# First norm's modulation in column blocks, with products against a 64-fold vector

## Chip, cores, metric

One core of one Trainium2 chip runs the whole kernel. The metric is device time in microseconds of one execution; about 1% is what a measurement of this kernel can tell from no change. Engines are named as in the profile: PE multiplies matrices (PEld is its loading of the stationary operand), DVE, ACT and POOL work on vectors, and SP issues nearly all transfers.

## The reference, cut to what matters

A block of a transformer with conditioned norms. A vector `c` of 512 gives six rows of modulation through `w_mod` (512 x 3072); the first norm uses the first two of them, a shift `sa` and a scale `ca`.

```python
mod = (_silu(c) @ w_mod).reshape(c.shape[0], 6, 1, -1)
sa, ca, ga, sb, cb, gb = (mod[:, i] for i in range(6))
h = _layernorm(x) * (1 + ca) + sa              # x: 1 x 2048 x 512
x = x + ga * _A_ref(h, wq, wk, wv, wo, beta)   # 32 heads, 4 segments of 512, with a memory
h = _layernorm(x) * (1 + cb) + sb
x = x + gb * _B_ref(h, w1, b1, w2, b2)         # 512 -> 1792 -> 512, squared relu
```

Inside `_A_ref` the first step is `q = h @ wq`, `k = h @ wk`, `v = h @ wv`.

## The kernel before

All work is written as nodes of a plan: `op(engine, cost, function, priority, after, get, put)`. Every engine has a hand-kept list `ORDER` of node numbers, and the plan sends each engine's instructions in the order of that list. An engine therefore waits at the head of its list even if something behind it could go. Synchronization between engines follows the tiles that instructions read and write.

The sequence is cut in four segments of 512 tokens. For the first one the start of the kernel goes like this.

- `silu` forms the vector `cs`, four columns of 128. Around it PE runs fillers (L566), products of zeros of 512 columns which compute nothing.
- `mod_cols` makes the scale. `mod_parts` loads 128 rows of `w_mod` at a time (L581), multiplies them with `cs` into four row groups (L588), ACT copies the row (L592), and four one-column products turn it into columns (L608), read out by DVE (L610).
- `mod_first` makes the shift. It loads four row blocks (L618) and makes four one-column products with each (L623), every 128 x 128 piece of `w_mod` being stationary once. DVE sums the parts (L629).
- `ln1` loads x (`load_x`, L698), takes statistics (L637, L638), finds the reciprocal deviation on POOL (L645, L646) and normalizes on DVE (L649).
- `ln_transposed` turns 256 tokens at a time (L658): PE transposes four 128 x 128 pieces a step into two PSUM banks, and an affine step applies scale and shift per channel, one chunk of 128 channels on ACT (L670) and the next on DVE (L672). The result is split into a high half (ACT, L678) and a low half (DVE, L680) of `HT`. Chunks 0 and 1 form one pair, chunks 2 and 3 the other. Every affine step waits for all of the scale and the shift (`MODC`).
- `split_w` loads `wk`, `wq` and `wv` (L740), the first 128 columns of each on their own, and splits them into halves (ACT L750, POOL or DVE L754).
- `qk(0)` is the first projection, three products per step (L786 to L788): for each of `wq` and `wk` and each half of the tokens four steps, one per channel chunk. The first step of a half waits for all four parts of `HT` of those tokens.
- Copies of the result (L833, L835) go to the tile `ST` by twelve transfers (L850), from which the scores (L908) are formed. The other groups of projections (L796), the memory and the value products follow, then the output projection and the second half of the block (L1514 to L1577).

Of the kernel before, what the change touches and what calls it, by code (L numbers as in the profile page):

```python
# [8 lines left out]
F32 = mybir.dt.float32  # L9
# [4 lines left out]
ALU = mybir.AluOpType  # L14
# [4 lines left out]
P = 128  # L19
D = 512  # L20
# [40 lines left out]
16 56 37 40 24 43 17 58 3 27 59 46 36 55 25 61 29 20 31 19 71 50 33-34 73 42 22 76 57 78 41 80 91 82 92 35 49 52 51  # L61
103 53 21 26 18 104 23 30 156 146 157 147-148 158-159 149 160 150-152 161 153 162-163 32 54 39 47-48 44 312-315 45 60
317-320 215 731-732 28 38 743-744 220 181 225 182-184 470-473 234 186 242 187-188 228 189 244 475-476 223 477-478
198-200 230 201 340 247 203-204 253 205-206 258 265 595-598 239 261 273 600-601 268 348 602-603 350 353 249 277 359
345 278 256 279 281 288 411 284 355 291 369 414 382 498 511 296 384 506 536 372 300-302 416 753 423 390 431 367 754
426 755-756 364 508 419 758-759 503 760 374 761 517 530 398 435-436 439 442 539 437 400 392 513 446 449 522 406 623
631 856 454 408 527 636 458-460 525 541 924 548 925 544 926 532 551 927 642 650 929 556 930-931 628 932 661 633
560-562 564 784-785 571 574 786-787 567 655 789 579 790 652 791 638 647 792 993 818 583-585 664 657 666 673 1061 669
1062 837 1063 831 1064 676 845 1066-1067 828 681 1068 860 1069 823 1346-1347 685-687 1358-1359 689 801-802 826 696 803
692 804 699 704 806-807 842 833 808 955 850 809 968 708-710 847 866 1198 873 1199 881 852 1200-1201 876 974 963  # L70
1203-1204 869 1205-1206 960 987 1130 885-887 863 889 965 979 896 892 997 970 899 1267 984 904 908 1092 1100 982
909-910 1003 1006 1105 989 1010 1013 1000 1097 1018 1022 1102 1368 1111 1023-1024 1026 1119 1369 1033 1370 1041 1371
1036 1029 1373 1124 1374 1107 1375 1229 1121 1376 1116 1045-1047 1399 1140 1400-1401 1143 1402 1134 1147 1404 1155
1242 1405 1126 1406 1150 1237 1407 1248 1159 1137 1234 1163 1160-1161 1166 1253 1539 1170 1540 1271 1541 1178 1239
1542 1471 1544 1173 1545 1258 1546 1244 1547 1433 1446 1274 1182-1184 1277 1261 1284 1961-1962 1973-1974 1292
1416-1417 1256 1418-1419 1280 1287 1421 1263 1422 1452 1441 1423-1424 1438 1608 1460 1296-1298 1457 1300 1676 1307
1677 1443 1303 1678-1679 1310 1465 1315 1681-1682 1448 1683 1475 1684 1570 1462 1319-1321 1478 1481 1578 1488
1813-1814 1491 1467 1815-1816 1589 1583 1484 1818-1819 1602 1496 1745 1820 1575 1612 1821 1580 1615 1500 1599 1504
1501 1507 1502 1511 1597 1514 1585 1519 1707 1882 1594 1523 1717 1618 1621 1524-1525 1720 1625 1604 1628 1712 1749
1633 1715 1726 1637-1639 1641 1648 1983 1739 1984 1656 1985 1722 1986 1644 1651 1734 1988-1990 1844 1857 1991 1849  # L80
1660-1661 1752 1662 2011 1852 1755 2012-2014 1762 1765 1854 2016-2017 1770 1731 2018 1859 2019 1736 1863 2145-2146
2083 1758 1873 2147-2148 1876 1868 2150-2151 1741 2152-2153 2045 1871 1774-1776 1778 2028 1781 2029 1785 1878 2030
1788 2031 1793 2064 2033 2058 1797-1799 1892 1899 2034 2050 2035-2036 1907 2053 2273-2274 1902 2275 2055 2276 2211
2278 2077 1895 2279 2069 2280 2060 2281 2074 2192 1911-1913 2072 1915 1922 1918 2205 1925 1930 2079 2197 1934 2173
2087 2200 1935-1936 2094 2097 2401 2178 2402-2404 2102 2090 2183 2406-2407 2186 2408-2409 2181 2339 2106 2188 2110
2113 1886 2107 2202 2117 2108 2120 2125 2301 2309 2129 1889 2215 2218 2314 2130-2131 2222 2207 2311 2225 2230 2320
2325 2234 2467 2235-2236 2238 2241 2306 2550-2553 2245 2248 2330 2561-2564 2316 2253 2328 2429 2333 2257-2259 2439
# [25 lines left out]
1 12 72 125 115 97 93 99 95 109 105 111 107 127 117 139 137 154 164 141 129 119 166 135 217 733 216 737 745 749 321
323 131 325 235-236 194 196 190-191 195 197 479 192-193 481 483 231-232 342 121 255 341 254 214 212 259 207 213 266
210-211 260 208-209 267 262 275 263 274 269-270 747 251 250 751 735 739 604 606 360 608 361 283 282 289 412-413 290
356 280 285-286 293 292 357 383 499 298 297 500 537-538 303 14 418 417 424-425 391 432-433 428 427 421 420 375-376 519
518 762 399 764 767 441 444 440 443 438 401 769 515 514 448 447 450-451 624 407 857 455-456 625 409 858 461 543 542
550 549 545 533-534 553 552 546 643 557-558 644 933 662 935 663 938 563 565-566 940 573 576 572 575 568-569 581 580
640 639 800 797 793 799 796 995 819 794 798 795 994 820 586 659 658 668 675 674 670 667 671 838-839 678 677 683 861
682 1070 862 1072 1075 1348 1352 688 1077 1364 690 1360 691 698 697 694 693 700-701 705-706 835 834 957 812 814  # L120
816-817 810 956 813 811 711 815 868 867 874-875 883 853 882 854 877 975 878 976 870-871 1207 1209 1350 1362 1131-1132
# [278 lines left out]
def block_kernel(ctx, tc, x, wq, wk, wv, wo, beta, w1, b1, w2, b2, c, wmod, out):  # L400
# [201 lines left out]
    def mod_cols(m, slot, plus, pr, after=(), pool="xr"):  # L602
# [3 lines left out]
        def mm():  # L606
            for k in range(KD):
# [3 lines left out]
                   pr + 0.05, after=[n], put=[b])  # L611

    def mod_first(m, slot, plus, pr):

        key, b = ("wmod", m), ("modc", m)
        n = None
        for k in range(KD):
# [1015 lines left out]
```

## Time and profile before

| what | value |
|---|---|
| median of 3 runs | 765.24 us (764.63 to 771.92) |
| profiled execution | 768.07 us |
| its span | 766.3 us |
| mean granted clock | 0.982 |
| PE busy | 739.7 us, 97% |
| DVE, ACT, POOL busy | 599.8, 501.1, 253.5 us |
| first projection begins | 23.38 us after the span's start |

In the profile's rows the first number is the start within the span and the second the time that the row took; a row can merge several neighbouring instructions, whose number stands behind the x. A name such as `bmodc` is a PSUM bank. What stands in brackets is the engine's idle time before the row and what ended it.

### The profile page before, as it was taken

The page shows a single profiled execution, that of the slowest core. Times are in us where ns is not written, and L with a number is a line of the kernel's source. Part 1 is how long each engine was busy: PE and PEld are TensorE (multiplying, and loading weights), DVE is VectorE, ACT ScalarE, POOL GpSimd, SP SyncE. Part 2 cuts the span into 40 slices and gives each one's busy share as a digit, 9 for nine tenths or more (in the row PEclk, how much of TensorE's full clock was granted, in tenths as well). Part 3 has the DMA queues.
Part 4 walks back from the last instruction along what each step waited for, and adds up shares of the span by engine and source line. Part 5 has one row for each costly group of instructions (what it writes and reads, how often), then busy time and mean ns, then how long its engine had stood idle before and what let it go on. Part 6 is the DMA issues. An engine that isn't in the chain of part 4 may idle for free.

```text
span 766.3 us, 17131 instructions
## 1 busy us (share of the span) xinstructions
PE 739.7 (97%) x6107; PEld 574.9 (75%) x6107; DVE 599.8 (78%) x1460; ACT 501.1 (65%) x977; POOL 253.5 (33%) x351
## 2 busy tenths in 40 slices
PE   9998999999999999999999599999999999999998
PEld 6776657776777667765565488889889898899886
DVE  4686788878997888688967999999968676776543
ACT  1547778889887896787867445667566455654541
POOL 4537245447765675565757230100000000000000
PEclk8999899999999999999999799999999999999999
DMA  9665667536665676658787868636533335233401
GB/s 304 176 153 131 191 182 219 151 100 172 187 182 149 187 201 167 179 154 223 224 226 228 257 207 278 193 127 198 165 123 115 114 110 165 66 108 123 124 1 56
DMA packets 102143, 126.72 MB, mean 165 GB/s; under 512 B 18981, under 2 KB 54569, under 8 KB 102058
## 3 DMA queue, kind: packets, MB, share of 16 engines
q1 hardware_dynamic: 101906, 125.49, 55.5%
q8 instruction: 49, 0.80, 0.4%
q14 instruction: 36, 0.29, 0.1%
q10 hardware_dynamic: 152, 0.13, 0.1%
HBM read 70.59 MB, written 27.99 MB: 129 GB/s over the span
## 4 chain that ended last, share of the span: by engine, by line
PE 77%; DVE 7%; ACT 5%; SPq 4%; issue 3%; DMA 2%; POOL 0%; DVEq 0%; ACTq 0%; POOLq 0%
PE bqk L796 8%; PE bpv L1127 6%; PE bpf L1577 6%; PE bpf L1576 6%; PE bpf L1575 6%; PE bv L875 5%; PE ba L908 5%; PE bpb L1068 5%; PE bhy L1514 3%; PE bhy L1516 3%; PE bhy L1515 3%; ACT pt L1085 3%; PE bhx L1516 3%; PE bhx L1514 3%; PE bhx L1515 2%
## 5 line engine op out<-in xcount | busy, mean ns | idle before, releaser
L913 DVE CUSTOM_DVE_ANT_0 ba<-ba,msk 128x384 f32<-128x384 f32 (+2 forms) x384 | 186.3, 542 | 40.0 <-PE ba L908 33.5
L1085 ACT ACTIVATE pt<-bpb 128x512 f32<-128x512 f32 x320 | 170.8, 615 | 23.9 <-PE bpb L1068 20.9
L796 PE MATMUL bqk<-HT,WQK 64*128 64x512 f32 x720 | 100.0, 397 | 0.2 <-DVE phi L843 0.2
L1072 POOL TENSOR_SCALAR_AFFINE_SELECT pt<-pt 128x512 f32<-128x512 f32 x128 | 79.5, 643 | 58.4 <-ACT pt L1085 52.2
L1460 ACT CAST ST<-SG 128x768 fp32r<-128x768 f32 (+1 forms) x56 | 52.3, 941 | 60.0 <-PE bhy L1515 56.4
L1577 PE MATMUL bpf<-W,ST 128*128 128x512 f32 x224 | 88.8, 396 | 0.5 <-DVE ST L1562 0.5
L1575 PE MATMUL bpf<-W,ST 128*128 128x512 f32 x224 | 88.9, 397 | 0.0
L1576 PE MATMUL bpf<-W,ST 128*128 128x512 f32 x224 | 88.6, 395 | 0.0
L1068 PE MATMUL bpb<-ST 64*128 64x256 f32 (+2 forms) x512 | 77.8, 351 | 6.6 <-DVE mx L913 1.8
L1127 PE MATMUL bpv<-pt,VT 128*32 128x512 f32 (+3 forms) x1024 | 79.3, 437 | 1.5 <-POOL pt L1072 0.7
L796 PEld LDWEIGHTS bqk<-HT,WQK 64*128 64x128 f32 x720 | 69.7, 185 | 12.4 <-issue 1.7
L908 PE MATMUL ba<-ST 63*128 63x256 f32 (+2 forms) x512 | 76.5, 349 | 0.9 <-DMA ST<-SG 0.3
L1068 PEld LDWEIGHTS bpb<-ST 64*128 64x128 f32 x512 | 51.8, 187 | 27.3 <-issue 4.4
L1463 DVE TENSOR_TENSOR ST<-SG,ST 128x768 fp32r<-128x768 f32 (+1 forms) x56 | 60.3, 1085 | 10.4 <-ACT ST L1460 10.4
L908 PEld LDWEIGHTS ba<-ST 63*128 63x128 f32 x512 | 50.8, 188 | 23.2 <-ACT pt L1085 5.1
L1213 POOL TENSOR_TENSOR X1L<-X1L 128x512 f32<-128x512 f32 x40 | 53.4, 1340 | 34.1 <-DMA X1L<-o_gate 28.1
L1553 ACT ACTIVATE AC<-AC,b1c 128x512 f32<-128x512 f32 x56 | 37.9, 718 | 29.1 <-DVE AC L1535 29.1
L1127 PEld LDWEIGHTS bpv<-pt,VT 128*32 128x32 f32 x1024 | 27.7, 109 | 37.9 <-issue 26.0
L875 PE MATMUL bv<-WVO,HT 64*128 64x512 f32 x384 | 55.8, 399 | 0.3 <-ACT xt L670 0.2
L1535 DVE TENSOR_TENSOR AC<-AC,bhy 128x256 f32<-128x256 f32 (+1 forms) x56 | 30.8, 550 | 30.7 <-PE bhy L1516 30.0
L913 DVE DVE_READ_ACCUMULATOR2_ANT mx<- 128x1 f32 x384 | 54.1, 141 | 0.0
L645 POOL TENSOR_SCALAR st_all<-st_all 128x4 f32<-128x4 f32 x4 | 1.4, 361 | 155.1 <-DVE st_all L638 155.1
(202 smaller groups left out, 1756.8 us busy)
## 6 DMA issues: line engine op xcount, KB each, us to landing
ST<-SG SPq DMA_DIRECT2D x192, 128.0 KB
SG<-s_dram SPq DMA_DIRECT2D x21, 512.0 KB
SG<-in_B_w SPq DMA_DIRECT2D x35, 256.0 KB
o_raw<-oraw SPq DMA_DIRECT2D x16, 512.0 KB
X1L<-o_raw SPq DMA_DIRECT2D x28, 256.0 KB
X1L<-o_gate SPq DMA_DIRECT2D x28, 256.0 KB
wm<-in_w_mod SPq DMA_DIRECT2D x20, 256.0 KB
xt<-in_A_x SPq DMA_DIRECT2D x16, 256.0 KB
```

Of the source, the lines that this page charges most:

```text
L796: m = nc.tensor.matmul(bank(("qk", u, w)), W3(w, k, x, cc * P, (cc + 1) * P)[z], HT[z, y, k], start=(ph == 0 and k == 0 and i == 0), stop= ...
L875: m = nc.tensor.matmul(bank(("v", s, t)), HT[z, x, k, t * P:(t + 1) * P], WVO[z, k, y], start=(ph == 0 and k == 0 and i == 0), stop=(ph == ...
L908: nc.tensor.matmul(dst[:, c0:c0 + n], ST[b:b + 63, 0, sl, qt * P:(qt + 1) * P], ST[b:b + 63, 1, sl, :n], start=True, stop=True)
L913: nc.vector.tensor_tensor_reduce(i, i, msk[:, 512 - n:], scale=1.0, scalar=-3e38, op0=ALU.add, op1=ALU.max, accum_out=o)
L1068: nc.tensor.matmul(dst, ST[b:b + 64, 1, sl, kb * P:(kb + 1) * P], ST[b:b + 64, 0, sl, q0:512], start=True, stop=True)
L1072: nc.gpsimd.affine_select(out=ap, in_=ap, pattern=[[0, ap.shape[1]], [1, P]], compare_op=ALU.is_ge, fill=0.0, base=0, channel_multiplier=-1)
L1085: ns = [act(512, lambda j=j: nc.scalar.activation(buf("PPP"[n], pt)[:, i + j], bank(keys[j]), AF.Exp, scale=0.25), pr[slot] + 0.01 + 0.001 ...
L1127: nc.tensor.matmul(bank(o)[32 * hq:32 * hq + 32, q0:q0 + src.shape[1]], v[:, a:a + 32], src, start=start, stop=stop, tile_position=(0, 32 ...
L1463: nc.vector.tensor_tensor(TL[kd][:, 1, o:o + b - a], raw(k)[:, a:b], TL[kd][:, 0, o:o + b - a].bitcast(F32), op=ALU.subtract)
L1575: nc.tensor.matmul(p, rh, FF["W2"][:, f, 0], start=(f == 0), stop=False)
L1576: nc.tensor.matmul(p, rh, FF["W2"][:, f, 1], start=False, stop=False)
L1577: nc.tensor.matmul(p, rl, FF["W2"][:, f, 0], start=False, stop=(f == NF - 1))
```

## The change

`mod_first` and the first use of `mod_cols` go. In their place `mod_block(j)` makes scale and shift of channel chunk j in one step, for j from 0 to 3. It loads the 128 columns of `w_mod` that belong to the chunk, one transfer each for shift and scale (256 KB in rows of 512 B), and adds up four products for each, with the 128 x 128 pieces stationary and the vector's column repeated 64 times as the moving side. One of the 64 equal result columns is read by DVE, which adds 0 or 1.

```diff
-    n_ca = mod_cols(1, CA, 1.0, PR0 + 0.1, pool="P")
-    n_sa = mod_first(0, SA, 0.0, PR0 + 0.2)
-    MODC = {CA: [n_ca, n_sa]}
+    one = const.tile([P, 2], F32, name="one")
+    nc.vector.memset(one[:, 0:1], 0.0)
+    nc.vector.memset(one[:, 1:2], 1.0)
...
+    NR = 64
+    def mod_block(j):
+        c = slice(j * P, (j + 1) * P)
+        ld = [sp(lambda m=m: nc.sync.dma_start(buf("P", keys_m[m])[:, :, c],
+                                               wmod[:, m * D + j * P:m * D + (j + 1) * P].rearrange("(k p) n -> p k n", p=P)),
+                 PR0 + 0.1 + 0.01 * j + 0.001 * m, 200000, get=() if j else [("P", keys_m[m])]) for m in (0, 1)]
+
+        def mm():
+            for m in (0, 1):
+                for k in range(KD):
+                    nc.tensor.matmul(bank(b_m)[:, NR * (2 * j + m):NR * (2 * j + m + 1)], TL[keys_m[m]][:, k, c],
+                                     cs[:, k:k + 1].to_broadcast([P, NR]), start=k == 0, stop=k == KD - 1)
+        n = pe("F", 1.0, mm, PR0 + 0.12 + 0.01 * j, after=[n_cs, *ld], get=() if j else [("#D", b_m)], put=keys_m, act=0.5)
...
+        return dve(2, lambda: nc.vector.tensor_tensor(modc[:, 0:2, j], bank(b_m)[:, 2 * NR * j:2 * NR * (j + 1):NR], one, op=ALU.add),
+                   PR0 + 0.13 + 0.01 * j, after=[n], put=[b_m])
+    MODC = {CA: [mod_block(j) for j in range(KD)]}
```

In `ln_transposed` the affine step of a chunk waits for that chunk's block alone, where the norm is the first one:

```diff
+        def need(k):
+            return MODC[sc][k:k + 1] if sc == CA else MODC[sc]
...
-            af = [op("ACT", 0.46, ..., after=[*n, *MODC[sc]], put=[b[j]]),
-                  op("DVE", 0.46, ..., after=[*n, *MODC[sc]], put=[b[j]])]
+            af = [op("ACT", 0.46, ..., after=[*n, *need(2 * j)], put=[b[j]]),
+                  op("DVE", 0.46, ..., after=[*n, *need(2 * j + 1)], put=[b[j]])]
```

In `qk(0)` the first step of a half waits for the first pair of channel chunks, and the third step (k = 2) for the other pair:

```diff
-                           after=[n] if k else [*ht, *(WN[w, cc] if s == 0 else []), *ends], get=() if k or i else [("#D", b)])
+                           after=[n, *(ht[2:] if k == 2 else [])] if k else [*ht[:2], *(WN[w, cc] if s == 0 else []), *ends], get=() if k or i else [("#D", b)])
```

The lists in `ORDER` are new. Since the plan now has one node less in its first hundred, every number behind it is one lower, and beyond that many neighbours have changed places through the whole kernel. At the start they now read as follows, in words.

- SP: the four loads of x; the loads of blocks 1 and 0; the first chunk of `wq`; those of blocks 3 and 2; the first chunk of `wk`; the rest of `wk` and of `wq`. Before: scale, x, shift, then the first chunks of `wk` and `wq`.
- PE: 31 fillers around the small transpose of the vector, block 0, block 1, two transpose steps, a filler, the third transpose step, block 3, the fourth transpose step, block 2, step k = 0 of the `wq` projection, six fillers, step k = 1, then steps k = 0, 1 and 2 of `wk` and the rest.
- DVE: statistics, four normalizations, read-out of blocks 1 and 0, affine of chunk 1, read-out of block 3, low half of the first pair, read-out of block 2, affine of chunk 3, two affines of the other 256 tokens, then the low half of the second pair.
- ACT: the cast of the `wq` chunk, affine of chunk 0, high half, affine of chunk 0 of the other tokens, the cast of the `wk` chunk, affine of chunk 2, and on.

More of the change, by code (lines that the diff above doesn't have):

```diff
@@ L66 @@
[L66 to L75, printed above, removed]
@@ new lines @@
+1012 1096 999 1021 1110 1367 1101 1022-1023 1118 1025 1368 1032 1369 1040 1370 1028 1035 1372 1123 1373 1106 1374 1228
+1375 1115 1120 1044-1046 1398 1139 1399 1142 1400-1401 1133 1146 1403 1154 1404 1241 1125 1405 1149 1236 1406 1247
+1136 1158 1233 1162 1159-1160 1252 1165 1538 1169 1539 1238 1270 1540-1541 1177 1470 1172 1543-1544 1243 1545 1257
+1546 1432 1445 1181-1183 1273 1276 1260 1283 1960-1961 1972-1973 1291 1415-1416 1255 1417-1418 1279 1286 1420 1262
+1421 1451 1440 1422-1423 1437 1607 1459 1295-1297 1456 1299 1675 1306 1676 1302 1677 1442 1314 1678 1464 1309
@@ new lines @@
+1680-1681 1447 1682 1474 1683 1461 1569 1477 1318-1320 1480 1577 1812 1487 1813 1490 1466 1814-1815 1588 1582 1483
+1817-1818 1601 1495 1744 1819 1574 1611 1820 1579 1499 1614 1598 1503 1500 1506 1501 1510 1596 1513 1584 1706 1881
+1518 1593 1522 1716 1617 1620 1523-1524 1719 1624 1603 1627 1632 1748 1711 1636 1725 1714 1637-1638 1640 1647 1982
+1738 1983 1655 1984 1721 1985 1643 1650 1733 1987-1988 1843 1989 1856 1990 1848 1659-1661 1751 2010 1851 1754
+2011-2013 1761 1853 1764 2015-2016 1730 1769 2017 1858 2018 1735 1862 2144-2145 1872 2082 2146-2147 1757 1867 1740
@@ new lines @@
+2149-2151 2044 1875 2152 1870 1773-1775 1777 2027 1780 2028 1784 1877 2029 1787 2030 2063 1792 2032 2057 1796-1798
+2049 1891 2033 1898 1906 2034 2052 2035 2272 1901 2273 2054 2274 1894 2275 2210 2277 2076 2278-2279 2068 2059 2280
+2191 2073 1910-1911 1914 1921 2071 1917 2204 1912 1924 1929 2196 2078 1933 2199 2172 2086 1934-1935 2177 2400 2093
+2096 2401-2403 2182 2101 2089 2405-2406 2185 2407-2408 2180 2338 2105 2187 2109 1885 2112 2106-2107 2116 2300 2201
+2119 2124 2308 2128 1888 2313 2214 2217 2129-2130 2310 2221 2206 2224 2229 2233 2319 2324 2466 2305 2234-2235 2237
@@ new lines @@
+2240 2549-2552 2329 2244 2247 2560-2563 2315 2252 2327 2332 2428 2256-2258 2438 2334 2342 2349 2345 2626-2629 2352
+2433 2361 2436 2357 2365 2582-2584 2593 2585 2594 2447 2441 2368 2362-2363 2455 2372 2443 2595 2375 2380 2596
+2571-2572 2452 2457 2460 2384-2386 2470 2573-2574 2473 2462 2477 2485 2480 2604-2605 2489 2493 2496 2490-2491 2500
+2503 2508 2606 2636-2637 2648-2649 2512-2514 2607 2615-2618 2862 2880 2802-2804 2864 2866 2805 2867 2870 2780-2782
+2872 2783 2873 2813-2814 2882 2815-2816 2791 2884 2792-2793 2885 2888 2991 2898 2988 2990 2890-2891 2794 2994 2989
@@ new lines @@
+1511 1514 1708 1707 1520 1519 1883 1882 1619 1618 1622 1621 1525 1626 1604-1605 1628 1625 1629 1634 1633 1964 1749
+1726-1727 1750 1639 1642 1641 1648-1649 1657 1656 1723 1722 1651 1645 1652 1644 1844-1845 1991 1993 1996 1662
+1755-1756 1763 1762 1766 1765 1771 1770 1860 1859 2023 2026 2020 1864 2024-2025 1863 2019 2022 2084 2021 2083 1742
+1759 1741 1758 2046 2153 2045 2155 2158 1776 1778-1779 1782 1781 1878-1879 1786 1785 1788-1789 1793-1794 2064-2065
+1799 1893 1892 1900 1907 1899 1908 2041-2042 2037 2043 2040 2038 1903 1902 1896 1895 2036 2212 2039 2211 2060-2061
@@ new lines @@
+3091 2759 3095 3103 3093 3124 3106 2984 2983 2985-2986 3097 3127 2770 2774 3130 3148 3119 3118 3120-3121 3151 3172
+3143 3142 3154 3144-3145 3346 3348 3175 3178 3350 3167 3196 3166 3168-3169 3202 3199 3352 3220 3190-3192 3362 3193
+3360 3223 3364 3244 3215 3214 3216 3226 3217 3247 3250 3370 3374 3376 3372 3238 3379 3239-3241 3382 3403 3385 3263
+3262 3264 3406 3265 3409 3427 3397 3430 3398-3400 3433 3451 3454 3422 3421 3423-3424 3623 3457 3627 3475 3478
+3445-3446 3625 3629 3447-3448 3481 3499 3469-3470 3502 3471-3472 3635 3523 3494 3526 3505 3637 3493 3495-3496 3639
@@ new lines @@
+1693 1583 1602 1326 1575 1581 1576 1615 1580 1599 1822 1592 1825 1600 1597 1827 1830 1594-1595 1717-1718 1720 1710
+1712 1715 1713 1729 1739 1530 1734 1857 1992 1850 1997 1849 1752 1995 1852 1847 1854-1855 1732 1731 1737 1736
+1873-1874 1667 1866 1869 1868 1876 1871 2159 2154 2157 2048 2058 2051 2050 2053 2067 2055-2056 1804 2077 2069-2070
+2075 2074 2282 2287 2285 2072 2205 2195 2197-2198 2200 2176 2178-2179 2184 2183 2186 2181 2415 2410 2529 2413 1941
+2203 2531 2533 2541 2202 2309 1889 2314 2304 2311 2537 2312 2326 2535 2325 2543 2539 2307 2136 2306 2330 2323 2553
@@ L228 @@
+2294 2292 2298 2293 2296-2297 1937 2291 2299 2081 1940 1938 2528 2532 2540 2545 2417 1939 2418 2341 2190 2536 1942
+2427 2416 2419 2423 1943 2546 2132 2424 2209 2425 1945 2133 2556 2578 2421-2422 2137 2579 2557 2420 2622 2426 2135
[8 rows of a table added]
 """,
@@ L611, in mod_cols @@
                    pr + 0.05, after=[n], put=[b])
[L613 to L617, printed above, removed]
-            ld = sp(lambda k=k: nc.sync.dma_start(buf("P", key)[:, k], wmod[k * P:(k + 1) * P, m * D:(m + 1) * D]),
-                    pr + 0.001 * k, 175000, get=() if k else [("P", key)])
-            def mm(k):
-                for j in range(KD):
-                    nc.tensor.matmul(bank(b)[:, KD * j + k:KD * j + k + 1], TL[key][:, k, j * P:(j + 1) * P], cs[:, k:k + 1],
-                                     start=True, stop=True)
-            n = pe("F", 0.9, lambda k=k: mm(k), pr + 0.02 + 0.001 * k, after=[n_cs, ld, n], get=() if k else [("#D", b)],
-                   put=[key] if k == KD - 1 else (), act=0.05)
-        def out_():
-            nc.vector.tensor_reduce(modc[:, slot, :], bank(b)[:, :KD * KD].rearrange("p (j k) -> p j k", k=KD), axis=AX.X, op=ALU.add)
-            if plus:
-                nc.vector.tensor_scalar(modc[:, slot, :], modc[:, slot, :], plus, None, op0=ALU.add)
-        return op("DVE", 0.15 if plus else 0.08, out_, pr + 0.05, after=[n], put=[b])
     def ln_stats(xt, mv):
@@ L680, in split @@
                     (nc.gpsimd if low == "POOL" else nc.vector).tensor_tensor(lo, fv, hi.bitcast(F32), op=ALU.subtract)
-            af = [op("ACT", 0.46, lambda f=affine: f("a"), pr + 0.01 + 0.001 * j, after=[*n, *MODC[sc]], put=[b[j]]),
-                  op("DVE", 0.46, lambda f=affine: f("v"), pr + 0.01 + 0.001 * j, after=[*n, *MODC[sc]], put=[b[j]])]
+            af = [op("ACT", 0.46, lambda f=affine: f("a"), pr + 0.01 + 0.001 * j, after=[*n, *need(2 * j)], put=[b[j]]),
+                  op("DVE", 0.46, lambda f=affine: f("v"), pr + 0.01 + 0.001 * j, after=[*n, *need(2 * j + 1)], put=[b[j]])]
             if bare:
@@ L701, in block_kernel @@
     load_x(0, PR0)
-    n_ca = mod_cols(1, CA, 1.0, PR0 + 0.1, pool="P")
-    n_sa = mod_first(0, SA, 0.0, PR0 + 0.2)
-    MODC = {CA: [n_ca, n_sa]}
+    one = const.tile([P, 2], F32, name="one")
+    nc.vector.memset(one[:, 0:1], 0.0)
+    nc.vector.memset(one[:, 1:2], 1.0)
+    n_blk = []
+    keys_m, b_m = [("wm", 0, 0), ("wm", 1, 0)], ("modc", 0)
+    NR = 64
[10 more added lines that the diff above has]
+        n = pe("F", 1.0, mm, PR0 + 0.12 + 0.01 * j, after=[n_cs, *ld], get=() if j else [("#D", b_m)], put=keys_m, act=0.5)
+        if j == 0:
+            n_blk.append(n)
+        else:
+            n_blk[0].outs.append(n)
+            n.left += 1
+        return dve(2, lambda: nc.vector.tensor_tensor(modc[:, 0:2, j], bank(b_m)[:, 2 * NR * j:2 * NR * (j + 1):NR], one, op=ALU.add),
+                   PR0 + 0.13 + 0.01 * j, after=[n], put=[b_m])
+    MODC = {CA: [mod_block(j) for j in range(KD)]}
     HTN = {}
```

254 lines of the change are left out of this document (114 added, 140 removed), and 17 rows, old and new, of the table ORDER.

## The prediction

> **What bounds the kernel now.** I read the page's busy shares and slices first, to see which engine sets the time.
>
> ```profile
> span 766.3 us, 17131 instructions
> PE 739.7 (97%) x6107; PEld 574.9 (75%) x6107; DVE 599.8 (78%) x1460; ACT 501.1 (65%) x977; POOL 253.5 (33%) x351
> PE   9998999999999999999999599999999999999998
> PEclk8999899999999999999999799999999999999999
> ```
>
> PE is busy for 739.7 of 766.3 us, so what the start of the kernel loses is not made up later: a stretch at the start counts almost one for one. The granted clock falls in slices 1, 5 and 23. The change lies in the first 30 us. So the chain that ended last comes next, in its first 24 us (start, us, what):
>
> ```profile
> 5.12 2.51 PE bwarm L566 x11
> 7.63 0.99 PE bmod L588 x8
> 9.41 1.05 PE bmodc L608 x8
> 10.91 1.02 PE bmodc L623 x8
> 12.24 1.50 PE bmodc L623 x8
> 14.19 1.50 PE bmodc L623 x8
> 16.64 1.50 PE bmodc L623 x8
> 18.14 0.96 PE blnq L658 x4
> 19.09 1.71 PE bwarm L566 x4
> 20.80 0.85 PE blnq L658 x4
> 21.65 1.21 PE bwarm L566 x4
> 22.86 0.44 PE blnq L658 x4
> ```
>
> It is PE all the way: the scale (L588, L608), the shift (L623), four transpose steps (L658, two more at 15.69 and 18.14), and warm-up fillers, which compute nothing. The same kind of step costs 1.02 us before 12 us and 1.50 after, for the reason that the view by windows gives (us, busy of each engine, granted clock, DMA share, GB/s):
>
> ```profile
> 7.50:10.90 3.40, 3.37 (x23) 1.40 (x22) 2.62 (x7) 0.58 (x1) 0.00 (x0) 1.00 1.02 385
> 10.90:12.20 1.30, 1.30 (x12) 1.25 (x11) 0.53 (x2) 0.00 (x0) 0.56 (x2) 0.91 1.03 344
> 12.20:15.50 3.30, 3.30 (x18) 3.21 (x17) 1.99 (x5) 1.24 (x2) 0.82 (x2) 0.50 1.12 342
> 18.20:23.30 5.10, 5.10 (x21) 3.17 (x21) 2.44 (x5) 2.16 (x4) 0.00 (x0) 0.61 0.66 229
> 23.30:28.80 5.50, 5.50 (x46) 5.42 (x45) 2.30 (x4) 4.25 (x8) 2.55 (x2) 1.00 0.54 182
> ```
>
> PE is never idle there, yet its clock is 0.50 through the one-column products, and 1.00 again in the first projections. Those start at 23.3, hold 48 products, and end where the next filler starts, at 29.37. The timeline shows what they wait for:
>
> ```profile
> 8.17 0.69 DVE L637 BATCH_NORM_STATS2 bs<-xt 128x6 f32<-128x512 f32 x1 [3.43 <-DMA xt<-in_A_x]
> 11.56 0.23 POOL L645 TENSOR_SCALAR mv<-mv 128x4 f32<-128x4 f32 x1 [6.18 <-DVE mv L638]
> 12.95 1.46 DVE L649 TENSOR_SCALAR xt<-xt,mv 128x512 f32<-128x512 f32 x3 [1.49 <-POOL mv L646]
> 13.82 0.62 ACT L750 CAST WQK<-w 128x512 fp32r<-128x512 f32 x1 [4.47 <-DMA w<-in_A_wk]
> 16.62 1.26 POOL L754 TENSOR_TENSOR WQK<-w,WQK 128x512 fp32r<-128x512 f32 x1
> 19.13 1.02 ACT L670 ACTIVATE xt<-blnq,modc 128x256 f32<-128x256 f32 x2 [3.81 <-PE blnq L658]
> 19.73 1.00 DVE L672 TENSOR_SCALAR xt<-blnq,modc 128x256 f32<-128x256 f32 x2 [1.38 <-ACT xt L670]
> 20.31 1.14 ACT L678 CAST HT<-xt 128x512 fp32r<-128x512 f32 x2 [0.16 <-DVE xt L672]
> 20.96 1.29 DVE L680 TENSOR_TENSOR HT<-xt,HT 128x512 fp32r<-128x512 f32 x2 [0.23 <-ACT HT L678]
> 29.37 1.47 PE L566 MATMUL bwarm<-wz 128*128 128x512 bf16 x6
> ```
>
> The affine step (L670, L672) waits for PE, not for data; from it to the low half of HT (L680) pass 3.1 us.
>
> **Loads.** All old modulation loads come before the weights; the first wk chunk is the thirteenth load of 256 KB.
>
> ```profile
> DMA packets 575, 1.04 MB, mean 187 GB/s; under 512 B 62, under 2 KB 66, under 8 KB 575
> DMA packets 2217, 3.39 MB, mean 273 GB/s; under 512 B 203, under 2 KB 681, under 8 KB 2217
> DMA packets 309, 0.16 MB, mean 325 GB/s; under 512 B 13, under 2 KB 302, under 8 KB 309
> ```
>
> These are the stretches 0 to 5.6, 0 to 12.4 and 12 to 12.5 us. The thirteen loads make 3.41 MB, moved by about 12.4 us, and ACT takes the chunk at 13.82: 1.4 us from last byte to first use. Rows of 512 B ran at 325 GB/s. The change moves the same 2.1 MB of modulation, now all in 512 B rows, and SP puts the four x loads first, the wq chunk ahead of half the blocks, the wk chunk behind all. With 1.04 MB in 5.6 us and, cautiously, 0.31 MB/us after it, plus 1.4: x at 7.0, block 0 at 9.5, block 1 at 10.4, wq chunk 11.2, block 3 at 12.9, block 2 at 14.6, wk chunk 15.5 (1.7 later than now). The rest of wk and wq slides back by the same order and is wanted only by the second group of projections. The statistics move ahead with x: four take 3.3 us, from 8.17 to the 11.5 of POOL's row, and POOL 1.4 more; with the last x at 7.0 the applies run from about 9.5 to 11.4. POOL and DVE have nothing else there.
>
> **PE's sum.** Out go one scale step (0.99), its transpose to columns (1.05), four shift steps (1.02 + 3 x 1.50): 7.56 us of PE, with an ACT copy and two short DVE steps. In come four blocks of 8 products, each of two instructions (the old 4 products of L608 stand as x8): 64 instructions, with four short DVE adds and two one-column memsets, which lie beside them. The trace has no 64-column fp32 product. From one side: one column, 128x128 weights, 1.05 / 8 = 0.131 each. From the other: 512 columns,
>
> ```profile
> 109.45 1.05 PE bmodr L1393 x2
> ```
>
> 0.525 each, which for 64 columns is 0.066. A transpose, 128 columns, took 0.44 / 4 = 0.11 at full clock. As 1 and 128 columns cost nearly the same, the weights set the pace; I take 0.122, a block at 1.95 us, and keep 1.05 and 2.1 as ends. In a sentence by itself: the Trainium skill, in TensorE: Matmul & The Clock Gate, section LDWEIGHTS (loading the stationary operand), gives the time as columns over 1.2 GHz, 107 ns for 128, which makes a block 1.7 us and the gain below 1.0 us larger; the one-column row, at 131 ns, is slower than that.
>
> The new PE list sets 22 fillers between the small transpose of the vector (about 5.1, as now) and block 0: 22 x 0.22 = 4.8, so block 0 starts at 9.95, its data just there. At full clock: block 0 to 11.9, block 1 to 13.85, two transpose steps 0.9, a filler 0.2, a third step to 15.4, block 3 to 17.4, the fourth step 17.85, block 2 to 19.8. Data are ahead each time (12.9, 14.6). The projections then start, but only four of their sixteen steps (k of the first two blocks) can go: 19.8, six fillers, done about 22.4. The wk chunk, on the way of its own (15.5 + 0.62 ACT behind an affine + 1.26 POOL), is there by about 20.5. The other steps wait for block 2: DVE reads it out by 20.1, ACT's affine 0.55, DVE's 0.55 (one after the other, as in the rows at 19.13 and 19.73), the cast 0.6; DVE's list has two affines of the other tokens before the subtraction, so that goes at 22.4 and ends at 23.1. Twelve steps of 0.36 (5.9 us / 16) then end at 27.6 instead of 29.37: 1.8 us won. Where the change promises overlap it is mostly paid back: DVE has block 3's read-out ahead of the first low half, and that holds k 0 until 18.4, while PE is busy with block 2 anyway.
>
> Behind it the list holds eight fillers instead of ten up to the last transpose of the second segment, 0.4 us, if SP's transfers of the first projections move up too; they do, as their reader is the same copy. That is 2.2 us: 768.07 (the execution's own time: 1.8 around the span) less 2.2 is 765.9. That execution lies 2.8 above the median, 765.24; from the median, **763.0 us**.
>
> **The rest of the lists** is renumbered and shuffled: of 1,188 PE entries common to both, 520 keep their place, 294 move by one, none by over 20. The largest stall keeps its neighbours on PE and DVE:
>
> ```profile
> PE bhx L1516 <- DVE ST L1463: 9.2, 2, 9.0
> 77.00:84.00 7.00, 7.00 (x66) 3.77 (x65) 4.50 (x13) 5.26 (x14) 1.85 (x3) 0.52 0.50 135
> ```
>
> I cost the shuffle at nothing, between minus and plus 3.4 us: a half-clock stretch like that of 77 to 84 us (7 x 0.48) lost or added.
>
> **Rivals.** *The clock stays at half* (slower side). It fell behind a stretch in which one-column products filled about half the time beside fillers, with PE busy throughout; what 64 columns count for no row shows. For it: their moving part, by the 0.066 above, fills only half of the 0.122. Against: the transposes and wide products at 1.00. At half clock from 12.0 to 22.2 a block is 3.0 (two rows of 1.50), block 1 ends at 15.0, block 3 at 21.3, block 2 at 24.1 and the projections at 31.8: 2.4 later, 2.0 with the two fillers, 767.2. It decides from a mean block of 2.5 us on. Chance 0.18. The same page of the Trainium skill, in its section The HAM clock gate, ties the clock to how busy PE was in windows of about 3.4 us; by that alone the old products, with PE busy throughout, would have kept the full clock, and the row of 0.50 speaks against reading it so.
>
> *Blocks are cheap*: at 1.05 us block 2 ends at 16.3, the later twelve steps start at 19.7 and end at 24.0, 5.4 earlier; with the fillers 759.4. For it: the row of 512 columns; against: the one-column row. Chance 0.17.
>
> *The start does not reach the end*: the shuffle adds or removes a stall of the size of the half-clock stretch; 759.6 to 766.4. Against it: 97% PE. Chance 0.15.
>
> **How the numbers follow.** My forecast, 760 to 766 alone, has 0.50. The cases together reach from 759.4 to 767.2; with half a half-clock stretch (1.7) on either end, rounded, 757.5 to 768.5. About 1% is what a measurement can tell from no change; under 757.6 needs cheap blocks and a stretch gone as well, 0.08; over 772.9 needs the half clock and two more stretches, 0.04; within, 0.88.
>
> **What would show it.** Right: clock 1.00 in 12 to 22 us; blocks of 16 instructions at 1.9 to 2.1 us; block 2 ending near 19.8; HT's subtractions for the second half near 23; the first projection's last step near 27.6. Wrong: granted clock 0.50 there, blocks near 1.05, block loads landing after PE is ready, or the gain gone by 40 us, or a stall elsewhere that now has none.

## The result, and the profile after

| | before | after |
|---|---|---|
| median of 20 runs each | 768.09 us (764.21 to 772.84) | 765.14 us (760.29 to 770.03) |
| ratio of the two, 95% interval | | 0.995 (0.9928 to 0.9971) |
| profiled execution, its span | 768.07, 766.3 us | 767.98, 766.1 us |
| its mean granted clock | 0.982 | 0.984 |
| start of the filler behind the first projection | 29.37 us | 26.38 us |

The change gains half a per cent: 2.95 us between the medians. Runs more than 1.5% above the fastest of their kernel are left out of all medians, ratios and means here; there were two, one of a_nr32 and one of the kernel before beside it. The gain is less than the 1% that the prediction took as its bound, but the interval of 20 runs on each side lies wholly below 1. The two profiled executions, on the other hand, are equal in length. So the profile must be read for where time moves, and the gain itself from the runs.

The page of the kernel after, its first lines (spans, engines, forty slices, granted clock in tenths):

```profile
span 766.1 us, 17116 instructions
PE 739.5 (97%) x6123; PEld 580.5 (76%) x6123; DVE 602.4 (79%) x1464; ACT 502.6 (66%) x976; POOL 255.5 (33%) x351
PE   9898999999999999999999599999999999999998
PEclk9999899999999999999999799999999999999999
```

PE's busy time is the same to 0.2 us, though the old products were replaced and their slow stretch is gone. Slice 1, which stood at 8 for the clock, now has 9; slices 5 and 23 stand as before. In PE's own row slice 2 has gone down from 9 to 8: PE is idle there for part of the time, as the windows below show.

The chain of the kernel after, in order of time (start, us, what):

```profile
5.25 5.11 PE bwarm L566 x22
10.36 3.52 PE bmodc L702 x32
13.88 0.88 PE blnq L639 x8
14.97 0.44 PE blnq L639 x4
15.41 1.73 PE bmodc L702 x16
17.15 0.45 PE blnq L639 x4
17.59 1.81 PE bmodc L702 x16
...
29.21 1.29 POOL WVO L763
30.62 0.24 POOL mv L623
30.93 1.05 POOL mv L624
```

Blocks 0 and 1 stand together as 32 instructions in 3.52 us, which is 0.110 us each. Blocks 3 and 2 took 1.73 and 1.81. The view by windows (us, busy of PE, PEld, DVE, ACT and POOL with counts, granted clock, DMA share, GB/s) has the clock:

```profile
12.20:15.50 3.30, 3.30 (x32) 3.21 (x31) 0.55 (x3) 0.56 (x1) 1.26 (x1) 1.00 1.17 304
15.50:18.20 2.70, 2.70 (x26) 2.65 (x26) 0.98 (x3) 1.41 (x3) 0.00 (x0) 1.00 1.05 370
18.20:23.30 5.10, 5.10 (x40) 4.44 (x40) 3.14 (x7) 3.44 (x7) 1.28 (x1) 1.00 0.37 112
...
28.80:38.00 9.20, 7.12 (x52) 4.74 (x52) 7.93 (x13) 3.25 (x7) 8.26 (x10) 1.00 0.80 224
173.00:183.00 10.00, 9.58 (x78) 5.17 (x80) 8.02 (x23) 8.63 (x21) 7.06 (x12) 0.83 0.51 136
262.00:272.00 10.00, 7.68 (x82) 3.30 (x74) 9.04 (x26) 6.93 (x16) 6.12 (x9) 0.83 0.60 182
```

From 12 to 23 us the clock is 1.00 where it was 0.50 to 0.61. From 28.8 to 38.0, however, PE is busy for 7.12 of 9.20 us; before it had been busy throughout. The last two rows hold new half-clock stretches of 3.4 us each. Before, the same three windows had PE without idle time in the first and a clock of 1.00 in all:

```profile
28.80:38.00 9.20, 9.20 (x72) 6.45 (x71) 7.47 (x15) 4.18 (x8) 7.19 (x9) 1.00 0.65 163
173.00:183.00 10.00, 9.45 (x88) 5.63 (x86) 9.40 (x32) 9.83 (x24) 7.54 (x13) 1.00 0.54 140
262.00:272.00 10.00, 8.10 (x70) 3.93 (x66) 8.58 (x24) 8.81 (x20) 8.07 (x11) 1.00 0.64 184
```

With the starts of the same PE instructions compared between the two traces (medians), the kernel after leads by 2.1 to 3.7 us from 25 to 125 us and by about 1 up to 175. The 2 us between go without any change of the clock: at 122.93 us PE waits 1.49 us for a transfer (L1077, `ST` from `mt`), where the kernel before has no wait. It is 1.3 behind after the stretch at 176 and 2.6 behind after that at 265. Between 360 and 425 us it catches up, and beyond 400 us the two lie mostly within 0.6 of each other. One execution thus shows the gain won and lost again, at a wait as well as in half-clock stretches; whether the loss belongs to the change needs more executions.

The timeline shows the steps that the prediction named:

```profile
21.33 1.29 DVE L661 TENSOR_TENSOR HT<-xt,HT 128x512 fp32r<-128x512 f32 x2 [0.38 <-ACT HT L659]
26.38 0.61 PE L566 MATMUL bwarm<-wz 128*128 128x512 bf16 x2
32.01 4.38 DVE L627 TENSOR_SCALAR xt<-xt,mv 128x512 f32<-128x512 f32 x4 [1.20 <-POOL mv L624]
32.74 2.86 POOL L763 TENSOR_TENSOR WVO<-w,WVO 128x512 fp32r<-128x512 f32 x2 [0.77 <-ACT WVO L759]
36.45 1.09 PE L639 MATMUL blnq<-ident,xt 128*128 128x128 f32 x8 [1.41 <-DVE xt L627]
```

PE waits 1.41 us for the second segment's normalizations at 36.45. In the chain above, POOL made the low half of a weight (L763, 29.21 to 30.50) before the reciprocal deviation on which they hang (L623, L624). The four normalizations then took 4.38 us beside POOL's next two subtractions. That, with a wait of 0.66 us at 30.59, is the first place where a part of the start's gain is given back.

### The profile page after: what moved, and what is told of

It is laid out like the page before. It is cut to its first block, busy times and chain, and to the rows that moved or that the text cites. A ratio compares the mean times of both kernels' runs of the same rounds, so it can differ in the third digit from the quotient of the medians.

```text
span 766.1 us, 17116 instructions
## 1 busy us (share of the span) xinstructions
PE 739.5 (97%) x6123; PEld 580.5 (76%) x6123; DVE 602.4 (79%) x1464; ACT 502.6 (66%) x976; POOL 255.5 (33%) x351
## 4 chain that ended last, share of the span: by engine, by line
PE 78%; DVE 6%; ACT 4%; DMA 4%; SPq 3%; issue 2%; POOL 2%; DVEq 0%; ACTq 0%; POOLq 0%
PE bqk L805 9%; PE bpv L1136 7%; PE bpf L1584 6%; PE bpf L1586 6%; PE bpf L1585 6%; PE bv L884 5%; PE ba L917 5%; PE bpb L1077 5%; PE bhy L1523 3%; PE bhy L1525 3%; PE bhy L1524 3%; PE bhx L1525 2%; PE bhx L1523 2%; PE bhx L1524 2%; ACT pt L1094 2%
## 5 line engine op out<-in xcount | busy, mean ns | idle before, releaser
L1094 ACT ACTIVATE pt<-bpb 128x512 f32<-128x512 f32 x320 | 169.0, 606 | 23.3 <-PE bpb L1077 22.3
L805 PE MATMUL bqk<-HT,WQK 64*128 64x512 f32 x720 | 102.3, 398 | 0.8 <-POOL hinge_s L530 0.7
L1077 PE MATMUL bpb<-ST 64*128 64x256 f32 (+2 forms) x512 | 79.0, 358 | 3.6 <-DMA ST<-mt 1.9
L805 PEld LDWEIGHTS bqk<-HT,WQK 64*128 64x128 f32 x720 | 73.0, 185 | 9.6 <-POOL hinge_s L530 1.7
L1077 PEld LDWEIGHTS bpb<-ST 64*128 64x128 f32 x512 | 53.2, 190 | 22.2 <-issue 5.7
L1571 DVE TENSOR_TENSOR ST<-AC,ST 128x1024 fp32r<-128x1024 f32 x28 | 34.3, 1224 | 20.3 <-ACT ST L1568 20.1
```

What stands on the lines that cost most here:

```text
L805: m = nc.tensor.matmul(bank(("qk", u, w)), W3(w, k, x, cc * P, (cc + 1) * P)[z], HT[z, y, k], start=(ph == 0 and k == 0 and i == 0), stop= ...
L1077: nc.tensor.matmul(dst, ST[b:b + 64, 1, sl, kb * P:(kb + 1) * P], ST[b:b + 64, 0, sl, q0:512], start=True, stop=True)
L1094: ns = [act(512, lambda j=j: nc.scalar.activation(buf("PPP"[n], pt)[:, i + j], bank(keys[j]), AF.Exp, scale=0.25), pr[slot] + 0.01 + 0.001 ...
```

## The experiments

The leading theory after these traces: the gain is the granted clock's, brought by products with 64 columns instead of one; the form in blocks, the work behind each chunk and the new lists bring nothing of their own. The rivals: the chunk-wise start makes the gain; or the shuffled lists do. Since one execution cannot tell, each further kernel was run 6 to 12 times, each set beside its own runs of the kernel before. For each run I split the span in two. *Lost* is the span times one minus the mean granted clock. *Rest* is the span less that. Over the 96 runs of the kernel before in these sets, a run with 1 us more lost is 0.89 us longer (correlation 0.84), so lost time makes most of the difference between runs of one kernel. It overstates a little, as half clock while PE idles costs nothing. For the runs of the kernel before in the result above the clock is not on record. Means over the runs:

| kernel | median us | ratio to before (95%) | lost us | rest us |
|---|---|---|---|---|
| before, beside these (96 runs) | 768.9 to 769.7 | | 14.8 (14.5 to 15.2 by set) | 753.0 |
| after (20 runs) | 765.14 | 0.995 (0.9928 to 0.9971) | 10.4 | 752.9 |
| after_again | 765.66 | 0.9943 (0.9914 to 0.9972) | 9.3 | 754.2 |
| a_nr1 | 773.78 | 1.0057 (1.0034 to 1.008) | 19.0 | 753.0 |
| a_nr16 | 772.18 | 1.0029 (1.0 to 1.0058) | 16.8 | 753.0 |
| a_nr32 | 767.43 | 0.9981 (0.9954 to 1.0008) | 12.3 | 753.7 |
| b_wide32 | 765.32 | 0.9941 (0.9912 to 0.9969) | 9.8 | 753.9 |
| a_oldtail | 765.83 | 0.9948 (0.9919 to 0.9977) | 9.5 | 755.0 |
| b_newtail | 771.39 | 1.0031 (1.0003 to 1.0058) | 13.6 | 756.2 |
| a_whole | 771.04 | 1.0007 (0.9981 to 1.0033) | 12.3 | 756.7 |
| a_whole_fill | 767.49 | 0.9976 (0.9949 to 1.0004) | 9.9 | 755.8 |
| a_fill (6 runs) | 761.55 | 0.9896 (0.9856 to 0.9936) | 3.7 | 756.4 |
| a_fill_again | 765.0 | 0.9936 (0.9904 to 0.9968) | 5.4 | 756.9 |
| b_wide32_fill | 766.19 | 0.9969 (0.9938 to 1.0) | 7.8 | 756.4 |

**How many columns.** The kernel after with 1 column (a_nr1), 16 (a_nr16) and 32 (a_nr32) in place of 64, all else equal; the diff of the first:

```diff
-    NR = 64
+    NR = 1
```

> The changed kernel with the vector's column once instead of 64 times (NR = 1), all else as it is. Theory 1 (the gain at the start comes from the clock that 64 columns hold): granted clock 0.50 for some 7 to 10 us between about 12 and 23 us, blocks 2 and 3 at 2.5 to 3.0 us instead of 1.8, last step of the first projection near 28.5 to 31 us instead of 26.4, ratio to before 0.998 to 1.002. Theory 2 (it comes from chunk-wise order alone, the clock being held by PE's being busy): clock 1.00, blocks at 1.8, projection's end at 26.4, ratio near 0.995. Theory 3 (it comes from the reshuffled later lists): ratio near 0.995 whatever the start does.

> The changed kernel with the column 16 times instead of 64. Where the columns count in proportion, it lies between 1 and 64: half clock in part of the runs, ratio 0.997 to 1.002. Where any few columns are enough, ratio 0.993 to 0.997 as with 64. Blocks take 1.7 to 1.8 us at full clock by both, as the weights set their pace.

> The changed kernel with the column 32 times. If what decides is the columns of the products against their pace, as 16 fell to half clock and 64 did not, 32 lies between: either ratio 0.993 to 0.997 and clock 1.00 to 60 us (enough), or 1.000 to 1.003 with a half-clock stretch between 12 and 30 us (too few). 32 columns in the kernel before were enough, but with fillers between the steps.

The lost time goes 19.0, 16.8, 12.3 and 9.3 (after_again) with 1, 16, 32 and 64 columns, and the rest stays at 753.0 to 754.2. With one or 16 columns the block form is no faster than the kernel before, and with one it is slower: 1.0057, above the 0.998 to 1.002 expected. With 32 it ties with the kernel before and lies between the two cases expected. The view by windows of a_nr16, and the timeline row of one of its blocks:

```profile
12.00:15.50 3.50, 3.50 (x24) 3.50 (x24) 0.23 (x2) 0.00 (x0) 0.75 (x1) 0.68 1.18 311
15.50:18.20 2.70, 2.70 (x14) 2.44 (x13) 0.54 (x1) 1.18 (x2) 0.00 (x0) 0.50 1.05 370
...
23.30:28.80 5.50, 5.50 (x21) 3.94 (x22) 2.81 (x6) 2.70 (x6) 0.85 (x1) 0.50 0.13 45
```
```profile
17.76 3.43 PE L702 MATMUL bmodc<-cs,wm 128*128 128x16 f32 x16
```

PE is busy in every microsecond, yet its clock is 0.50, and a block of 16 instructions takes 3.43 us instead of 1.90 in the same view of the kernel after. The half-clock stretch runs from 13.2 us for 17.1 us, so the first projection ended at 34.73. With one column it began at 18.3 and lasted 6.8 us, with 32 at 18.5 and 3.4 us, here in the windows of a_nr1 and a_nr32:

```profile
15.50:18.20 2.70, 2.70 (x27) 2.70 (x26) 0.76 (x2) 1.50 (x3) 0.09 (x1) 1.00 1.06 370
18.20:23.30 5.10, 5.10 (x19) 3.54 (x19) 3.30 (x7) 3.31 (x7) 1.18 (x1) 0.51 0.34 93
```
```profile
18.20:23.30 5.10, 5.10 (x27) 3.71 (x27) 3.19 (x7) 3.20 (x6) 1.27 (x1) 0.67 0.34 84
```

With 1 and 32 columns the clock falls late, during the last block, so that it is mainly the fillers and products behind the narrow ones that run slowly. That the runs with one column were worse than those with 16, although its projection ended at 29.03, is not settled by the start: its profile has half clock for 13.7 us each at 79.7 and 434.7, against 6.8 and 10.2 with 16 columns. Whether that belongs to one column or to this execution stays open.

**Width without blocks.** The kernel before with its old shift products widened, its order untouched:

```diff
-  nc.tensor.matmul(bank(b)[:, KD * j + k:KD * j + k + 1], ..., cs[:, k:k + 1],
+  nc.tensor.matmul(bank(b)[:, 32 * (KD * j + k):32 * (KD * j + k + 1)], ..., cs[:, k:k + 1].to_broadcast([P, 32]),
...
-  nc.vector.tensor_reduce(modc[:, slot, :], bank(b)[:, :KD * KD]..., axis=AX.X, op=ALU.add)
+  nc.vector.tensor_reduce(modc[:, slot, :], bank(b)[:, 0:512:32]..., axis=AX.X, op=ALU.add)
```

> The kernel before, its shift products with the vector's column 32 times instead of once (one PSUM bank holds 16 x 32 columns), lists unchanged. Theory 1: clock 1.00 between 12 and 22 us if 32 columns are enough, shift steps at 1.0 instead of 1.5 us, first projection's end near 26.5 to 27.5 instead of 29.4, ratio 0.996 to 0.998; if 32 are too few, half clock as before and no change. Theories 2 and 3: half clock or not, no change of the time, 1.000.

It ties with the whole change: 0.9941 against 0.995 and 0.9943, lost 9.8 us. That is a larger gain than the 0.996 to 0.998 that theory 1 expected of it. Its windows, and the timeline row that begins behind its first projection:

```profile
12.00:15.50 3.50, 3.50 (x33) 3.45 (x32) 2.02 (x6) 1.24 (x2) 1.00 (x2) 1.00 1.12 339
18.20:23.30 5.10, 5.03 (x41) 4.60 (x40) 3.15 (x6) 4.29 (x9) 1.86 (x2) 1.00 1.01 358
```
```profile
24.85 1.04 PE L566 MATMUL bwarm<-wz 128*128 128x512 bf16 x4
```

The clock holds, and the projection ends even 1.5 us earlier than with the blocks. Two edited lines therefore bring what the change brings.

**The lists.** The later part of `ORDER` (everything behind the first hundred and sixty-odd nodes) in the sequence of the other kernel; here the first place on PE's list that differs, in the numbers of each kernel:

```diff
  a_oldtail
-... 317 318 730 731 47 29 39 61 37 742 ...
+... 317 318 319 214 47 29 39 61 37 730 ...
  b_newtail
-... 318 319 320 215 731 732 28 38 743 744 ...
+... 318 319 731 732 743 744 28 38 320 215 ...
```

> The changed kernel, with everything behind the first 165 nodes in the sequence of the lists of before (numbers one lower), the start as changed. Theories 1 and 2: the gain stays, ratio 0.994 to 0.997, first projection's end at 26.4. Theory 3: ratio 0.999 to 1.001.

> The kernel before, with everything behind its first 166 nodes in the changed kernel's sequence. Theories 1 and 2: ratio 0.999 to 1.001, half clock between 12 and 22 us as before. Theory 3: ratio near 0.995.

> The changed kernel as it is, beside the other kernels of this set: ratio 0.993 to 0.997. By the theory that the gain is the granted clock's, the mean span times the mean share of clock lost is 4 to 5 us below that of the kernel before, and the rest of the span is equal within 1 us.

The change with the old lists behind its start is as fast as the change (0.9948; after_again, the change unchanged, 0.9943). The new lists alone, on the old start, gain nothing: 1.0031, by its interval just slower. The shuffle is not the source of the gain. after_again also answers the third expectation: against the kernel before of its own set the lost time falls from 15.2 to 9.3 us, a little more than the 4 to 5 expected, and the rest rises from 753.0 to 754.2, a little more than the 1 us allowed.

b_newtail's profile shows one thing more. Its start is the kernel before's, yet the first projection ended at 26.35 us, not 29.37. The windows of b_newtail:

```profile
12.20:15.50 3.30, 3.30 (x31) 3.21 (x30) 1.98 (x5) 1.18 (x2) 0.90 (x1) 1.00 1.11 344
15.50:19.10 3.60, 3.60 (x15) 2.18 (x14) 2.23 (x5) 2.21 (x5) 2.50 (x2) 0.53 1.07 376
19.10:23.30 4.20, 4.20 (x33) 3.71 (x32) 2.39 (x5) 2.82 (x6) 0.06 (x1) 1.00 0.78 282
```

The same one-column products as before cost 3.4 us of half clock here (15.7 to 19.1), and 10.2 us in the profile before (12.0 to 22.2). What they cost thus differs between executions, and the profile before held the longer stretch; how often each comes two executions do not say. In the profiles of the seven kernels with wide products and full clock through the start (after, after_again, a_oldtail, a_fill, a_fill_again, b_wide32, b_wide32_fill) the first 60 us hold no half clock at all. So the old start loses 5.1 and 1.7 us there, the wide ones none, of the 4.4 to 5.9 us of lost time by which the means of the change and of the kernel before differ.

**Work behind each chunk.** The change with the projection's first step waiting for all four chunks, in the order k = 2, 3, 0, 1 (the marks of the first and last product of a sum move with it, not shown); and the same with the six fillers, which stand between its first two steps, moved ahead of it:

```diff
-  n = pe("F", 0.699 / 2, lambda ...: mm(w, k, b, c), ..., after=[n, *(ht[2:] if k == 2 else [])] if k else [*ht[:2], ...
+  n = pe("F", 0.699 / 2, lambda ...: mm(w, (k + 2) % KD, b, c), ..., after=[n] if k else [*ht, ...
  a_whole_fill, PE's list
-103 77 145 28 56 25 50 41 24 146
+103 77 28 56 25 50 41 24 145 146
```

> The changed kernel, the first projection's steps in the order of chunks 2, 3, 0, 1, so that none can begin before the last pair of chunks is there: the projection no longer runs behind each chunk. Clock theory: clock still 1.00 to 60 us, the projection ends 1.4 to 1.8 us later (near 28) and its time is at most 1.5 us above the changed kernel's, ratio 0.995 to 0.997. The rival, that working behind each chunk makes the gain: ratio 0.999 to 1.001.

> The changed kernel with the chunk order 2, 3, 0, 1 as in the run before, and the six fillers that stood behind the projection's first step now ahead of it, so that PE is not idle for 2.5 us while it waits for the last pair. If the loss of that run came by idle time and the clock after it: clock 1.00 to 60 us, projection's end near 28, ratio 0.995 to 0.998. If the overlap with the chunks is itself worth the 4 to 5 us: ratio 0.999 to 1.002 again with clock 1.00.

Without the fillers PE stood idle before the projection, and the clock fell in it. The windows of a_whole:

```profile
18.20:23.30 5.10, 2.81 (x20) 2.22 (x20) 3.00 (x7) 3.43 (x8) 1.26 (x1) 1.00 0.30 95
23.30:28.80 5.50, 5.50 (x31) 4.87 (x30) 1.57 (x3) 1.13 (x3) 2.51 (x2) 0.69 0.91 303
```

PE is idle for 2.3 of the first 5.1 us, the next window has 0.69 of the clock, the projection ends at 31.1, and the gain is gone (1.0007). That is the ratio that the rival had expected, but idle time and lost clock came in with it, so this run alone does not decide. With the fillers the projection ends at 28.10, some 2 us behind the change (26.07 and 26.38), and the ratio is 0.9976 against 0.9943, with intervals that overlap. This is within the clock theory's range, though the clock was not 1.00 to 60 us as expected: 3.4 us of half clock begin at 37.0. Within the block form the early steps are thus worth up to 2 us, not clear of the spread. Against the old form they are worth nothing that can be seen, since b_wide32 does without.

**The largest stall.** If lost clock is the currency, the next lot lies where PE idles for want of the second part's inputs, at about 425 us. The edit puts 32 fillers ahead of the product that waits there; `wz` is zeros, and the bank is written anew afterwards:

```diff
+  for _ in range(32):
+      nc.tensor.matmul(bank(x)..., wz, wz[:, None, :].to_broadcast([P, 4, P]), start=True, stop=True)
```

> The changed kernel with 32 fillers of 512 columns (6.8 us at full clock) ahead of the first product of the second half of the block, where PE idles 7.4 us near 425 us and then works at clock 0.50 to 439 us. Theory (idle time costs by the clock that follows): clock 1.00 through 425 to 440 us, 2 to 3 us less than the changed kernel, ratio 0.990 to 0.993. Rival: the products there wait for DVE and not for the clock, ratio 0.994 to 0.997; or the fillers themselves end later than the wait, slower.

> The changed kernel with the 32 fillers near 425 us once more, as what the kernel before with wide products and fillers is set against: ratio 0.987 to 0.993.

> The kernel before with its shift products 32 columns wide and the 32 fillers near 425 us. Theory (both gains are the clock's, the blocks add nothing): ratio within 0.003 of the changed kernel with the same fillers, 0.987 to 0.993. Rival (the blocks and the work behind each chunk have a worth of their own): ratio 0.004 or more above it.

The windows of the kernel after, then those of a_fill:

```profile
425.00:429.00 4.00, 0.00 (x0) 0.00 (x0) 3.90 (x8) 0.39 (x1) 1.95 (x2) 1.00 1.00 262
429.00:433.00 4.00, 0.80 (x3) 0.81 (x4) 3.93 (x7) 1.35 (x2) 0.00 (x0) 0.50 0.94 275
433.00:440.00 7.00, 5.94 (x21) 4.88 (x21) 5.06 (x10) 2.53 (x4) 0.00 (x0) 0.55 0.87 282
```
```profile
425.00:429.00 4.00, 4.00 (x21) 1.97 (x19) 3.93 (x9) 1.35 (x2) 0.00 (x0) 1.00 0.97 287
429.00:433.00 4.00, 1.51 (x11) 1.10 (x10) 3.86 (x8) 1.80 (x3) 0.00 (x0) 1.00 1.05 302
433.00:440.00 7.00, 7.00 (x45) 6.29 (x45) 6.43 (x14) 2.72 (x5) 0.00 (x0) 1.00 0.79 232
```

In both, PE is mostly idle from 429 to 433. The clock of 0.50 there, and of 0.55 behind it, becomes 1.00, and 45 products instead of 21 pass between 433 and 440. Over the runs the lost time falls from 9.3 to 3.7 and 5.4 us, while the rest grows by 2 to 3 us; that part of the half clock had covered idle time is a likely reason, not a tested one. Of its two sets, one gives 0.9896 and one 0.9936, against 0.9943 for the change. It is the fastest kernel here, by 3.6 and 0.5 us beyond after_again (the ratios' differences times 769); with intervals that overlap, how much of it is real is not settled. On b_wide32 the same edit shows no gain (0.9969 with, 0.9941 without). It lies 0.0033 above a_fill_again, between the 0.003 of the theory and the 0.004 of its rival.

## Why the prediction was right, and where its steps were off

The time fell inside the range with the sign forecast: 763.0 was said, 765.14 came. In the difference, -2.2 us was said and -2.95 came. The distance of 2.1 us in the absolute time is the base: three runs had a median of 765.24, and twenty of the same kernel 768.09, which is 2.85 more, and 0.75 of it is made up by the larger gain. Two of the prediction's sums do not come out as written, without weight for the result: 23.1 and twelve steps of 0.36 give 27.4, not 27.6, and 767.2 with 1.7 gives 768.9, not 768.5.

- **Full clock between 12 and 22 us, which decides the sum: right.** The clock is 1.00 there. The runs with fewer columns show that the products' width does it.
- **The half-clock rival** describes what the narrower forms do. It was priced at 767.2, 2 us above the base taken; a_nr1 came out 0.57% above its own base, which is 4.4 us (0.0057 x 769.2). It is decided by the columns, not by a block of 2.5 us: in a_nr1 the clock fell although its four blocks took 1.9 us in the mean (3.63, 1.84 and 2.27 us for the four in the timeline). The prediction weighed the section The HAM clock gate of the Trainium skill (TensorE: Matmul & The Clock Gate), by which the clock follows how busy PE is. If busy means what the profile counts, the traces disagree: a_nr16 had PE at 100% and a clock of 0.50. The same section has the clock decided in windows of about 3.4 us that run on their own and do not start with the kernel. With that the traces agree: stretches last 3.4, 6.8, 10.2, 13.7 and 17.1 us, and one start lost 3.4 in one execution and 10.2 in another.
- **The block: 0.122 us an instruction was said, 0.110 came** (3.52 / 32). Here the figure of the Trainium skill (TensorE: Matmul & The Clock Gate, LDWEIGHTS), 107 ns for 128 columns, was nearer than the one-column row. The fillers ahead took 5.11 us where 4.8 was said, so block 0 began at 10.36, not 9.95. The last block ended at 19.40 (17.59 + 1.81); 19.8 was said.
- **The low half of the second pair** was put at 22.4 to 23.1. It is the first of the two in the row at 21.33, done by about 22.0 (half of its 1.29 us). The prediction had set the two affines of the other tokens in front of it as time of their own; DVE made all three affines from 19.51 to 20.95 while ACT was still at its affine and the high half. PE then never waited in the projection: from the last block's end, six fillers and sixteen steps of 0.36 fill the time to 26.38 (19.40 + 1.2 + 5.8). The prediction had twelve steps wait until 23.1 and end at 27.6. So 3.0 us were won against 1.8.
- **Behind it 0.4 more was to be won; instead 0.7 was given back.** At the end of the second segment's transposes the lead was 2.3 us: 39.85 to 37.54, where the row before reads

```profile
38.81 1.04 PE L658 MATMUL blnq<-ident,xt 128*128 128x128 f32 x8
```

Six products of the second group (0.89 us) stand behind that place in the new list and ahead of it in the old one; from 50 to 60 us, where both have them done, PE's instructions lead by 2.25 us in the median. The 2.2 us of the prediction's sum is thus met by two errors that cancel. The missed term is DVE's normalizations beside POOL's subtractions: 4.38 us for four, where the second segment's before and the first segment's after took

```profile
35.55 2.88 DVE L649 TENSOR_SCALAR xt<-xt,mv 128x512 f32<-128x512 f32 x4 [0.90 <-POOL mv L646]
9.27 2.13 DVE L627 TENSOR_SCALAR xt<-xt,mv 128x512 f32<-128x512 f32 x4 [1.48 <-POOL mv L624]
```

POOL ran two subtractions beside the first of these three groups, one beside the second and none beside the third. That they are the cause is read from this alone; no run moves them.

- **That the start's gain reaches the end one for one: not shown.** In the profiled execution the lead was lost in three steps of about 2 us each, at the wait near 123 us and in the half-clock stretches at 176 and 265 us; behind the last it stood 2.6 us behind and came back to level by 425 us. Over the runs the gain is there, but as clock: beside its own set's kernel before, after_again loses 9.3 us instead of 15.2, and the rest is not lower (754.2 and 753.0). The prediction took one execution's 10.2 us of half clock at the start as the kernel's own; b_newtail's 3.4 us shows that it varies. That the sum nevertheless came near is then partly luck. The two profiles with the old start lose 5.1 and 1.7 us there; how much of the mean difference that makes, and how much lies in later stretches that shift with the start, stays open, since only one execution of each kernel was profiled.
- **The shuffle at nothing: right for the change** (a_oldtail 0.9948, after_again 0.9943).
- **Blocks cheap** (759.4) did not come: a block is 1.8 us, not 1.05.

## What to carry to other kernels

Keep small products wide enough to hold the clock: here a column repeated 32 times, with fillers between the steps, costs two edited lines and gains what a rebuilt start with 64 gains; in blocks one behind the other, 32 was not clearly enough (0.9981). Where PE must wait some microseconds, products of zeros can keep the clock for the work behind; what that is worth in time is not settled here. Before a profile's half-clock stretch is counted as a gain to be had, look at several executions' mean granted clock, for the place and length of such a stretch change from one to the next.

## What was not expected of the hardware

- Products with 1 or 16 columns of fp32 brought the clock to 0.50 with PE 100% busy; with 32 columns, in blocks, it fell for 3.4 us, and spread between fillers (b_wide32) it held; with 64 it held through the start in the profiles of after, after_again, a_oldtail, a_fill and a_fill_again.
- The runs of one kernel spread over 10 us, 760.29 to 770.03 for the change, and go with the mean granted clock, 0.978 to 0.990.
- The same DVE operation on 512 columns took from 543 to 2019 ns within one group, beside POOL's subtractions. In the view of the tile, the minimum, median and maximum stand behind the count:

```profile
L627 DVE TENSOR_SCALAR xt<-xt,mv x4: 543/1035/2019, 32.0 to 34.4; 128x512 f32<-128x512 f32 x4
```

- Loads in rows of 512 B moved at 290 GB/s, rows of 2 KB at 405; the views of the transfers, 9 to 13 us after and 9 to 11 us before:

```profile
DMA packets 2334, 1.16 MB, mean 290 GB/s; under 512 B 70, under 2 KB 2334, under 8 KB 2334
```
```profile
DMA packets 443, 0.81 MB, mean 405 GB/s; under 512 B 48, under 2 KB 48, under 8 KB 443
```

The blocks' loads were on time all the same: PE's chain has no wait for a transfer up to the end of the first projection.
